# AV of batch 0 over two banks, batch 1's inputs in another order, and five small loads inside a tanh loop: a fused pooling attention and MLP

One core of one Trainium2 chip. The metric is device time in microseconds (us) of one execution.

## The reference

```python
def _attn_ref(q, k, v):                      # [8, 8, 576, 64] float32
    k_p = k.reshape(B, H, Sp, 8, D).mean(axis=3)      # 576 keys pooled to 72
    v_p = v.reshape(B, H, Sp, 8, D).mean(axis=3)
    scores = np.matmul(q, k_p.transpose(0, 1, 3, 2)) / np.sqrt(D)
    attn = softmax(scores)
    return np.matmul(attn, v_p)

def _moe_ref(x, w_in, w_out):                # x [4608, 512], w_in [512, 2048], w_out [2048, 512]
    h = x @ w_in
    return (h - np.tanh(h)) @ w_out
```

The attention's output, heads put side by side, is x. (The softmax is written out in the full reference.)

## The kernel before

TensorE (PE) is the bound. Tokens go through the MLP in nine groups of 512. A group is 64 "h" matmuls (each of 16 tiles: four matmuls, a tanh on ScalarE, a subtraction on VectorE) and 64 "o" matmuls. The attention of batch b + 1 is threaded between the o matmuls of earlier groups; batch 0's stands alone in front. Words used below: AV is the product of attention weights and v; a *turn* is a transpose on PE; a *bank* is a piece of PSUM, where matmuls leave their result (one h tile, 512 float32 columns, fills one in this kernel); the *q tail* is the last 64 rows of a batch's q, *leftovers* are the last 16 of the 144 rows in which k and v are laid out, and both are loaded apart from the main part; kd is the pooled k. The *granted clock* is the share of TensorE's full clock that the profile records as granted. The parts that matter (lines starting with `# ...` stand for code left out):

```python
# GpSimd's stream: the weights, by quarters (w1 all four, w2 two of four)
for c in range(4):
    load_w1(c)
load_w2(0)
nc.gpsimd.tensor_copy(out=v_bf[:, NM, :], in_=v_raw[1][:, NM, :])
load_w2(1)
# ... memsets ...
q_raws[1] = raw.tile([128, H, R + 1, D], FP32, name="q_raw", tag="q_raw")
after(load_k(1), w1_dmas[1])     # SP's stream: batch 1's k, once w1's second quarter is there
load_q(1, False)                 # q without its tail of 64 rows
load_main(v_pairs, v_raw[1], 1, 0, NM)
# ... batch 0: k pooled, q turned, scores, v pooled ...
load_left(v_pairs, v_raw[1], 1, nc.scalar)    # ScalarE's stream: batch 1's v leftovers (four loads)
load_q_tail(1, q_raws[1], nc.scalar)          # and q tail (one load)
# ... AV of batch 0: eight halves of one bank, then the opening of h ...
for i in range(5, NHID):         # the h loop of group 0
    mlp_h(0, i, gts)             # four matmuls, tanh (ScalarE), subtraction (VectorE)
    # ... tail of batch 0's attention at i = 7, 9, 11, 13
pool_k(1, nc.gpsimd, mid=(2, 3)) # w2's quarters 2 and 3 are issued in the middle
after(load_k(2), w2_dmas[2])     # SP's stream: batch 2's k, once w2's third quarter is there
load_v(2)
load_q(2)
# ... the o loop of group 0, with batch 1's attention in it
```

One half of AV in batch 0: three matmuls into one bank, a reciprocal over 4 columns, a product over 256.

The softmax here doesn't subtract the row's maximum and nothing guards it: scores larger than these inputs give would overflow.

## Time and profile before

| | before |
|---|---|
| time, median (range) | 300.62 us (300.56 to 300.81), 3 runs |
| profiled span, granted TensorE clock | 299.1 us, 1.00 |
| PE busy | 291.5 us |
| batch 0's q tail on PE | 26.02 us |
| first o matmul | 34.55 us |
| batch 1's k turned | 37.82 us |

The last three are starts on PE, from its timeline; the prediction shows the lines of the last two. From the third on PE is never without work until the tail of the kernel, so whatever delays one of them delays the end. One more view: ScalarE's timeline in the front. Columns: start, length, engine (ACTq is ScalarE's sequencer issuing a transfer), line, operation, and in brackets the idle time before it with what ended it.

```profile
13.23 1.76 ACTq L106 DMA_DIRECT2D v_raw<-in_v_dram  x4
16.28 0.62 ACTq L127 DMA_DIRECT2D q_raw<-in_q_dram  x1
...
21.90 3.21 ACT L439 ACTIVATE t_sb<-hT_ps 128x512 f32<-128x512 f32 x6 [0.26 <-PE hT_ps L428]
```

The five small loads are issued at 13.23 to 16.9 us, before the tanh work begins. None waits for a large transfer. But one does wait: the first four are issued by 15.0, the fifth only at 16.28. In the built program it waits for batch 0's q tail (128 KB, issued at 8.12, landed 8.1 us later), and the first copies of a turned x, which stand behind it on ScalarE, start at 16.95, 1.0 us after PE has turned the first (15.99).

### The profile page before, as it was taken

How to read it: one execution, taken by the hardware profiler on the slowest of the kernel's cores; microseconds unless marked ns; L12 is line 12 of the kernel's file. 1: busy time of each engine (PE TensorE's matmuls, PEld its weight loads, DVE VectorE, ACT ScalarE, POOL GpSimd, SP SyncE). 2: the span in 40 equal slices, each digit the busy share in tenths (PEclk: the TensorE clock that was granted, in tenths of full speed). 3: DMA queues.
4: the chain of work that ended last, by engine and by line, in shares of the span. 5: the costliest groups of instructions: out<-in, count | busy, mean ns of one | idle time of the engine just before them, and what ended most of it. 6: DMA issues, size and time to landing. Idle time of an engine off the chain costs nothing.

```text
span 299.1 us, 4694 instructions
## 1 busy us (share of the span) xinstructions
PE 291.5 (97%) x1671; PEld 142.5 (48%) x1671; DVE 159.1 (53%) x343; ACT 149.4 (50%) x283; POOL 115.5 (39%) x110
## 2 busy tenths in 40 slices
PE   7989999999999999999999999999999999999994
PEld 3454455544544454445444554455445544444443
DVE  5658665673547444753476247716680758108600
ACT  4647583666146633654265516650665166126511
POOL 8500904871496109922971089307940000000000
PEclk9999999999999999999999999999999999999999
DMA  7999999849854998699648974897431430111032
GB/s 251 226 211 278 311 227 310 263 87 328 234 113 99 271 297 134 117 302 245 107 88 235 300 167 94 242 294 159 97 66 35 95 92 0 37 70 36 0 72 70
DMA packets 66183, 49.79 MB, mean 166 GB/s; under 512 B 39920, under 2 KB 52976, under 8 KB 66160
## 3 DMA queue, kind: packets, MB, share of 16 engines
q1 hardware_dynamic: 58832, 42.94, 56.0%
q0 software_dynamic: 4752, 4.72, 9.4%
q10 hardware_dynamic: 2576, 1.84, 2.3%
q8 instruction: 13, 0.21, 0.3%
q14 instruction: 10, 0.08, 0.1%
HBM read 36.70 MB, written 9.44 MB: 154 GB/s over the span
## 4 chain that ended last, share of the span: by engine, by line
PE 85%; DMA 9%; POOL 4%; issue 0%; SPq 0%; ACT 0%; DVE 0%; POOLq 0%
PE o_ps L456 40%; PE hT_ps L428 37%; DMA w1b<-in_moe_w_in_dram 4%; PE x_ps L346 4%; DMA k_raw<-in_k_dram 4%; PE s_ps L298 3%; POOL k_raw L198 1%; DMA out_dram<-o_sb 1%; POOL k_raw L203 1%; POOL kd L206 1%; POOL w2b L510 0%; PE xT_ps L390 0%; POOL v_raw L576 0%; PE qT_ps L171 0%; POOL w1b L503 0%
## 5 line engine op out<-in xcount | busy, mean ns | idle before, releaser
L456 PE MATMUL o_ps<-w2b,gT 128*128 128x512 bf16 x560 | 134.4, 380 | 0.0
L441 DVE TENSOR_TENSOR gT<-hT_ps,t_sb 128x512 bf16<-128x512 f32 x144 | 98.9, 691 | 57.7 <-ACT t_sb L439 57.6
L428 PE MATMUL hT_ps<-xT,w1b 128*128 128x512 bf16 x576 | 126.9, 379 | 0.3 <-ACT xT L397 0.3
L439 ACT ACTIVATE t_sb<-hT_ps 128x512 f32<-128x512 f32 x144 | 85.6, 597 | 38.3 <-PE hT_ps L428 37.5
L428 PEld LDWEIGHTS <-w1b 128*128 128x128 bf16 x576 | 55.9, 98 | 66.5 <-issue 0.4
L456 PEld LDWEIGHTS <-gT 128*128 128x128 bf16 x560 | 52.5, 98 | 52.0 <-issue 1.4
L465 ACT COPY o_sb<-o_ps 128x512 f32<-128x512 f32 x33 | 19.3, 585 | 75.2 <-PE o_ps L456 75.2
L359 DVE RECIPROCAL rden<-x_ps 128x4 f32<-128x4 f32 x80 | 14.2, 177 | 52.5 <-PE x_ps L346 52.0
L360 DVE TENSOR_TENSOR x_sb<-x_ps,rden 128x256 bf16<-128x256 f32 x80 | 34.0, 425 | 3.5 <-DMA xT<-x_sb 0.6
L148 POOL CAST q_bf<-q_raw 128x2048 bf16<-128x2048 f32 x6 | 11.3, 1888 | 59.9 <-issue 34.8
L198 POOL TENSOR_TENSOR k_raw<-k_raw 128x1280 f32<-128x1280 f32 x7 | 20.2, 2886 | 27.4 <-DMA k_raw<-in_k_dram 16.6
L317 ACT ACTIVATE E<-s_ps 128x288 bf16<-128x288 f32 x60 | 21.4, 410 | 13.2 <-PE s_ps L298 13.0
L346 PE MATMUL x_ps<-VB,E 128*128 128x130 bf16 x240 | 20.8, 221 | 0.4 <-ACT xT L397 0.3
L346 PEld LDWEIGHTS <-E 128*128 128x128 bf16 x240 | 16.9, 98 | 8.8 <-DVE VB L230 0.6
L216 POOL TENSOR_TENSOR v_raw<-v_raw 128x1280 f32<-128x1280 f32 x6 | 17.4, 2898 | 0.0
L298 PE MATMUL s_ps<-qT,KB 128*128 128x288 bf16 (+5 forms) x128 | 17.0, 290 | 0.2
L298 PEld LDWEIGHTS <-KB 128*128 128x128 bf16 (+1 forms) x128 | 7.0, 96 | 10.2 <-issue 3.5
L527 PE MATMUL warm_ps<-xT 128*128 128x512 bf16 x29 | 10.2, 465 | 1.3 <-DVE xT L539 1.3
L206 POOL TENSOR_TENSOR kd<-k_raw 128x640 bf16<-128x640 f32 x7 | 10.8, 1540 | 0.5
L203 POOL TENSOR_TENSOR k_raw<-k_raw 128x640 f32<-128x640 f32 x7 | 10.8, 1541 | 0.5
L397 ACT CAST xT<-xT_ps 128x256 bf16<-128x256 f32 (+1 forms) x14 | 5.8, 436 | 8.5 <-PE xT_ps L390 5.1
L219 POOL TENSOR_TENSOR v_raw<-v_raw 128x640 f32<-128x640 f32 x6 | 9.3, 1544 | 0.5
(73 smaller groups left out, 100.7 us busy)
## 6 DMA issues: line engine op xcount, KB each, us to landing
k_raw<-in_k_dram SPq DMA_DIRECT2D x7, 1024.0 KB, 5.9
q_raw<-in_q_dram SPq DMA_DIRECT2D x7, 1024.0 KB, 10.2
v_raw<-in_v_dram SPq DMA_DIRECT2D x7, 1024.0 KB, 9.3
out_dram<-o_sb SPq DMA_DIRECT2D x38, 128.0 KB, 2.4
out_dram<-o_sb SPq DMA_DIRECT2D x16, 256.0 KB, 3.7
w1b<-in_moe_w_in_dram POOLq DMA_DIRECT2D x4, 512.0 KB, 14.2
w2b<-in_moe_w_out_dram POOLq DMA_DIRECT2D x4, 512.0 KB, 16.9
k_raw<-in_k_dram SPq DMA_DIRECT2D x7, 128.0 KB, 5.8
```

What stands on the lines that cost most here:

```text
L198: first = eng.tensor_tensor(out=r[:, :, 0:4, :], in0=r[:, :, 0:4, :], in1=r[:, :, 4:8, :], op=ALU.add)
L216: eng.tensor_tensor(out=r[:, :, 0:4, :], in0=r[:, :, 0:4, :], in1=r[:, :, 4:8, :], op=ALU.add)
L298: nc.tensor.matmul(dst[p : p + w], lhsT=KB[b % 2][:, o : o + w], rhs=qTs[b][:, m, c0:c1], start=True, stop=True,)
L317: nc.scalar.activation(out=E[:, t, half * hs : (half + 1) * hs], in_=ps[:, :], func=ACT.Exp, scale=SCALE)
L346: nc.tensor.matmul(ps[:, 2 * n : 2 * n + 2, :].rearrange("p h d -> p (h d)") if n < 2 else ps.rearrange("p (a s) d -> p a s d", s=2)[:, :, ...
L359: nc.vector.reciprocal(out=rden[:, :, :], in_=ps[:, :, D:D1])
L360: nc.vector.tensor_tensor(out=x_sb[:, half, :, :], in0=ps[:, :, 0:D], in1=rden[:, :, :].to_broadcast([128, 4, D]), op=ALU.mult,)
L428: nc.tensor.matmul(h_tiles[i][:, :], lhsT=w1b[:, fb, i * 128 : (i + 1) * 128], rhs=xT[:, fb, tok0 : tok0 + TG], start=(fb == 0), stop=(fb ...
L439: nc.scalar.activation(out=t_sb[:, :], in_=h_ps[:, :], func=ACT.Tanh)
L441: nc.vector.tensor_sub(out=gT[:, :], in0=h_ps[:, :], in1=t_sb[:, :])
L456: nc.tensor.matmul(o_ps[:, :], lhsT=gts[i][:, tb * 128 : (tb + 1) * 128], rhs=w2b[:, i, :], start=(i == 0), stop=(i == NHID - 1),)
L465: (nc.vector.tensor_copy if g == 0 and tb % 2 else nc.scalar.copy)(out=o_sb[:, :], in_=o_ps[:, :])
```

## The change

Its intent: spend fewer VectorE instructions in batch 0's AV, which sets the pace of the front; ask for batch 1's k earlier and let no w2 transfer slow it; and take the five small loads off ScalarE where ScalarE now has part of the v pooling and the turns of x to do. Cut to its core (PSUM is also taken as one tile with banks given out by hand, which adds no instruction):

```diff
 # AV of batch 0: two blocks per step, over two banks; v placed by halves (VectorE, ScalarE)
-    av_half(0, 0, 0, xs[0], ps_all)          # eight of these, one bank each
+    av_pair(0, 0, 0)                         # four of these: 6 matmuls into two banks,
+                                             # one reciprocal (8 columns), one product (512)
-    x_pe_transpose(0, 0, xs[0], (0, 2))      # eight, each with a copy of 256
+    x0_turn((0, 1), 0, 7, nc.scalar.copy)    # two blocks per copy
 # batch 1's inputs
     for c in range(4):
         load_w1(c)
-    load_w2(0)
-    load_w2(1)
-    after(load_k(1), w1_dmas[1])
+    k1 = load_k(1)
+    after(k1[:1], w1_dmas[0])
+    load_w2(0)
+    after(w2_dmas, k1[0])                    # w2 held until batch 1's k is there
+    load_w2(1)
+    pool_k(1, nc.gpsimd)
+    load_w2(2)
+    load_w2(3)
 # five small loads of batch 1
-    load_left(v_pairs, v_raw[1], 1, nc.scalar)
-    load_q_tail(1, q_raws[1], nc.scalar)
     for i in range(5, NHID):
         mlp_h(0, i, gts)
+        if i in (5, 7, 9, 11):
+            load_left(v_pairs, v_raw[1], 1, nc.scalar, ((i - 5) // 2,))
+        if i == 13:
+            load_q_tail(1, q_raws[1], nc.scalar)
-    pool_k(1, nc.gpsimd, mid=(2, 3))
     after(load_k(2), w2_dmas[2])
```

## The prediction

> **What bounds the kernel now.** I read the page first: PE is busy for 291.5 of 299.1 us at full granted clock, so only PE's idle stretches and the work that fills time (the warm-up matmuls) can give anything back. Then the chain of waits in order of time, to see where the end is set by something other than PE:
>
> ```profile
> 5.17 0.69 POOL w1b L503
> 5.86 12.86 DMA w1b<-in_moe_w_in_dram
> 18.73 0.38 SPq L102
> 19.21 10.84 DMA k_raw<-in_k_dram
> 30.21 2.90 POOL k_raw L198
> 33.11 1.47 POOL w2b L510 x2
> 34.58 1.58 POOL k_raw L203
> 36.23 1.55 POOL kd L206
> 37.82 0.45 PE kT_ps L259 x5
> ```
>
> Columns are start, length, and what. From 37.82 us to the end the chain is PE alone, piece touching piece. So the change can move only what lies before 37.82, and the end moves by as much as that point moves. The chain there is a chain of transfers: second quarter of w1 landed (18.73), batch 1's k asked for, landed at 30.1, pooled on POOL with two w2 issues in the middle, and only then can PE turn k. The timeline of PE shows how little PE loses there:
>
> ```profile
> 20.41 5.78 PE L428 MATMUL hT_ps<-xT,w1b 128*128 128x512 bf16 x26
> ...
> 34.55 2.75 PE L456 MATMUL o_ps<-w2b,gT 128*128 128x512 bf16 x12
> 37.82 0.45 PE L259 MATMUL kT_ps<-ident,kd 128*128 128x128 bf16 x5 [0.52 <-POOL kd L206]
> ```
>
> The wait for kd is 0.52 us, all that the k part can return by itself. The other candidate is the time before 20.41, where PE reaches its unbroken run of h matmuls: there the chain of batch 0's attention (k, scores, v, AV, turned x) sets the pace, and the timeline of DVE shows AV as eight pairs of a reciprocal and a product:
>
> ```profile
> 14.13 0.76 DVE L230 TENSOR_TENSOR VB<-v_ps,mask 128x256 bf16<-128x256 f32 x2 [0.81 <-PE v_ps L618]
> 15.00 0.18 DVE L359 RECIPROCAL rden<-x_ps 128x4 f32<-128x4 f32 x1
> 15.22 0.42 DVE L360 TENSOR_TENSOR x_sb<-x_ps,rden 128x256 bf16<-128x256 f32 x1
> ...
> 19.63 0.43 DVE L360 TENSOR_TENSOR x_sb<-x_ps,rden 128x256 bf16<-128x256 f32 x1
> ```
>
> DVE is nearly full from 15.00 to 18.93, then waits 0.47 us and ends AV at 20.06. The last thing to read is how long weights take, by the view of the tile w2b:
>
> ```profile
> L510 POOL DMA_DIRECT2D w2b<-in_moe_w_out_dram x4: 747/764/780, 8.1 to 33.8; - x4
> ...
> DMA to landing us min/median/max: 8.7/16.9/24.4
> ```
>
> (issue times in ns, first and last start, then the time to landing). Asked in narrow windows about each issue, the view of transfers gives each landing: w1's quarters land 10.3, 12.9, 15.5 and 19.1 us after their issue, so at 15.46, 18.73, 22.1 and 26.5; w2's at 31.4, 35.7, 41.8 and 44.3. The first quarter of w2 lands 3.2 us before the o stage asks for it at 34.55.
>
> **What the Trainium skill says.** "DMA: Bandwidth & Descriptors", section Queues, rings and completion order: each DMA engine serves the queues it has work for in turn, packet by packet. The trace agrees: counting packets per us, the weight queue has 170 to 205 when alone, and 94 beside 94 of k's 2 KB packets from 24 to 28 us. So k does not overtake w1; it halves it. The same page, Specifications, gives first-byte latencies of about 0.6 us (SP, ACT) and 1 us (POOL); the trace does not agree here: k asked for at 18.73 moves its first bytes at 22.8 (4.1 us), and the third w2 quarter, issued at 33.05, at about 37.4 (4.3 us). I use the trace's. "VectorE: DVE Perf Modes", section on the TRN2 errata, gives a read of PSUM 120 + N cycles at 0.96 GHz: 392 ns for 256 elements, 658 for 512; the trace has 425 and 691. So a product over two banks saves one fixed share. "PSUM — Partial Sum Buffer", the section on bank collisions, asks for semaphores by bank; the built program agrees in that the first AV pair (banks 0 and 1) waits for ScalarE, which still reads half of v in bank 1.
>
> **The change part by part.**
>
> AV on DVE: removed 8 x (177 + 425) ns, added 4 x (about 180 + 691). With the gaps of the timeline one old half takes 0.545 us from start to start, one new pair about 0.90, so 4.36 becomes 3.6 us. The wait of 0.47 before the eighth goes too, since before the last pair PE has only one turn of x to do.
>
> Start of AV: the pooled v in halves lets DVE place the first half while PE pools the second; ScalarE places the second in two activations of 128 elements (estimate 0.25 us each, from 0.37 for 256 and 0.58 for 512). But E of the leftover rows is now computed after the first v half: scores at about 13.0, its exp over at about 14.0, ScalarE's two v pieces at 14.55. First AV pair done 14.95, against 15.00 for the first old half. Nothing gained at the start; the halves only make up for waiting on two blocks. DVE then ends AV at about 18.6 instead of 20.06.
>
> Turning x: ACT evacuates three tiles (two of 512, one of 256) and DVE one, where ACT had eight of 256. That is off the path.
>
> The opening of h: five tiles open with two matmuls each (10 x 0.216 us). The order is now 3, 4, two turns, 2, 0, 1. Tile 4 needs the second quarter of w1, which lands at about 18.6 as before. So 4 opens at 18.6 to 19.0, the turns take 0.25, three tiles 1.3: the openings are done at 20.55, and the remaining 22 matmuls before batch 0's q tail take 4.75, which puts the q tail at 25.3. Before, the timeline of PE has it at 26.02. **AV and opening give 0.7 us**, and PE would be ready for o at 33.85 instead of 34.55.
>
> Batch 1's inputs: k is now asked for after the first quarter of w1 (15.46), so 3.3 us earlier, moves from 19.5, shares with w1 at 94 packets per us, and its 512 main packets are through at 25.0, landed (1 us later, as in the trace) at 26.0. The last quarter of w1 lands at about 27.2 (26.5 before); it is asked for near 29.5, so no wait. POOL issues two w2 quarters from 26.0 and pools k in 6.1 us from 27.5 to 33.7: kd is ready before PE turns k, and the 0.52 us are gone.
>
> The price: the first quarter of w2 is issued at 26.0 instead of 8.05. Its bytes move from 26.0 + 4.3 = 30.3. The SP queue holds behind k the q of batch 1 and, newly, all of its v, because v's issue no longer waits for k to land. Counting packets from 19.5: q's 1024 small ones end at about 29.1 (122 per us beside w1, 338 alone), v has sent 230 by 30.3, its other 282 and w2's first 282 take 3.0 us at 94 each, and w2's last 230 take 1.2 alone: 34.5, landed near **35.4**. PE is ready at 33.85, so this is a new wait of 1.55 us. Then 12 o matmuls (2.59) and k is turned at 38.05, against 37.82: a loss of 0.2 us, the AV gain wholly hidden.
>
> The small loads of v's leftovers and q's tail go into ScalarE's h stretch, one issue of 0.43 us beside a tanh of 0.60 in periods of 0.87; PE has three banks there, so I give them 0 to 0.2 us.
>
> **The rivals.**
>
> First, w2 in time. The path through the w2 landing is long and each part is uncertain: if SP's latency falls to 2 or 3 us because the weight queue is shorter, k lands near 24.5, w2 moves from 28.5 and shares with q instead of v, and lands near 33.7. Then neither wait is there: 0.7 + 0.52 = 1.2 us faster, 299.4. For it speaks that someone chose this order on purpose; against it that all three transfers issued beside a deep weight queue took about 4 us to begin.
>
> Second, w2 later still, at 36.5, if the transfers share worse than counted: 1.3 us slower, 301.9.
>
> Third, the front gains nothing because opening tile 4 so early puts PE behind the second w1 quarter, or gains more (1.5 us) if v's halves start AV earlier. While w2 is late neither shows in the time.
>
> A fourth, PE losing its clock in the longer idle, I hold unlikely: the view by windows grants 1.00 in every stretch of before, and the new idle is under 2 us.
>
> **Range and chances.** I weigh the late w2 (300.6 + 0.2 = 300.8, spread 0.9) at 0.6 and w2 in time (299.4) at 0.4: 0.6 x 300.8 + 0.4 x 299.4 = 300.2. Range 299.0 to 301.6. A change of 2% is 6 us; the whole stretch that can move has 0.52 us of k wait and a front of 20 us whose chain stays, so faster 0.01, same 0.98, slower 0.01.
>
> **What would show it.** The chain of waits should name w2b's transfer between 26 and 35.5 in place of k_raw and POOL; the wait for kd should be gone; the first o matmul should start after 35, with idle before it put down to the w2b transfer; the q tail should start near 25.3; DVE's last AV product should end near 18.6. If the first o matmul starts at 33.9 with no idle, the first rival holds. The prediction is wrong if w2 lands before 33 or after 37, if PE stalls in the h stretch on w1 or on tanh, or if the time after the turn of k is no longer PE alone.

## The result and the profile after

Measured: **325.41 us** median (324.61 to 326.33, 4 runs) against 300.69 (300.56 to 300.81, 4 runs) before. The ratio is 1.082, with a 95% interval of 1.079 to 1.086. Ratios here are the mean time of one kernel's fast runs over that of the other's of the same rounds, so not quite the ratio of the medians. The prediction was 300.2 (299.0 to 301.6) with slower at 1%: wrong.

The profiled span is 322.9 us at a mean clock of 0.966, 23.8 us over before. PE's timeline shows where most of it sits:

```profile
25.28 1.02 PE L460 MATMUL PS<-xT,w1b 128*128 128x512 bf16 x4
48.48 1.86 PE L460 MATMUL PS<-xT,w1b 128*128 128x512 bf16 x4 [22.17 <-DVE gT L473]
...
57.73 2.54 PE L488 MATMUL PS<-w2b,gT 128*128 128x512 bf16 x11
```

PE stops in the middle of group 0's h tiles for 22.17 us, at 26.3. The first o matmul starts at 57.73 in place of 34.55, so 23.2 us of the 23.8 arise before it. The bracket names a VectorE subtraction: the next h tile has no free bank. The view of waits takes it back a step:

```profile
DVE gT L473 <- ACT t_sb L471: 81.8, 133, 22.5
...
ACT t_sb L471 <- DMA k_raw<-in_k_dram: 23.0, 1, 23.0
PE PS L460 <- DVE gT L473: 22.2, 1, 22.2
```

Columns: who waited for whom, us in total, how often, the longest. VectorE waited 22.5 us for one tanh, and that tanh waited 23.0 us, once, for a **k load**. A tanh reads no k. ScalarE's timeline shows what stands before it in ScalarE's stream:

```profile
46.65 0.36 ACTq L129 DMA_DIRECT2D v_raw<-in_v_dram  x1
47.10 1.09 ACT L471 ACTIVATE t_sb<-PS 128x512 f32<-128x512 f32 x2 [22.97 <-DMA k_raw<-in_k_dram]
50.60 0.32 ACTq L129 DMA_DIRECT2D v_raw<-in_v_dram  x1
```

The first small load goes out only at 46.65 and the second at 50.60; the tanhs behind each in ScalarE's stream start only after it, at 47.10 and 51.03. The chain of waits continues from the second one:

```profile
41.72 8.87 DMA v_raw<-in_v_dram
...
50.60 0.32 ACTq L129
```

The k load that ended at 46.6 was issued on SP, by the sync engine's timeline, at 41.02 (5.6 us to landing by the view of transfers):

```profile
41.02 0.58 SPq L134 DMA_DIRECT2D k_raw<-in_k_dram  x1
```

The v load at 41.72 landed at 41.72 + 8.87 = 50.6. Both are **batch 2's**. Its k is held until w2's third quarter has landed, at 40.5, and its v stands behind k in SP's stream. So a small load of batch 1 waited for large loads of batch 2.

The built program says why. Each transfer issued by SP or ScalarE signals its landing on one of eight semaphores, handed out in turn along one list of all engines' instructions. Each landing adds 16, and a transfer is issued only once its semaphore's previous user has landed (by a wait of its own, unless an earlier wait already covers it). This is the part of the list that matters, read from the built program of after (not a profile):

```
issuer   load                            signals   first waits for
SP       batch 2, k, 128 rows            DMAHW4    ... third w2 quarter
ScalarE  batch 0, q tail                 DMAHW5
SP       batch 2, k, remaining rows      DMAHW6
SP       batch 2, v, 128 rows            DMAHW7
SP       batch 2, v leftovers (4 loads)  DMAHW0 to 3
SP       batch 2, q (2 loads)            DMAHW4, 5
ScalarE  batch 1, v leftover 0           DMAHW6    DMAHW6 >= 32: batch 2's k remaining rows
ScalarE  batch 1, v leftover 1           DMAHW7    DMAHW7 >= 32: batch 2's v
ScalarE  batch 1, v leftover 2           DMAHW0    DMAHW0 >= 48: batch 2's v leftover
ScalarE  batch 1, v leftover 3           DMAHW1    DMAHW1 >= 48: batch 2's v leftover
ScalarE  batch 1, q tail                 DMAHW2    DMAHW2 >= 48: batch 2's v leftover
```

In the text of the kernel the small loads come before batch 2's. In this list they come behind. The Trainium skill, "DMA: Bandwidth & Descriptors", section on why a DMA increments its semaphore by 16, explains what the wait is for: with two transfers in flight on one semaphore, part of one's signals can pass for the other's. It asks for "One semaphore per in-flight slot, not one per stream." The waits in this program keep that rule, and the trace shows what they cost.

The rest of the 23.8 us. From q tail to first o, before takes 34.55 - 26.02 = 8.53 us and after 57.73 - 25.04 = 32.69: 24.16 more, 22.17 of which is the stop. The clock record of the trace shows most of the other 2.0: the clock is at half from 31.3, within the stop, for 20.48 us. The page's slices (8.07 us each) show it:

```profile
PE   7992009989999999999999999999999999999995
...
PEclk9999557999999999999999999999999999999999
```

PE works at half rate from 48.48 to 51.8, which costs 1.7 us. Some 0.3 us is not accounted for. The q tail is 1.0 us earlier in this run; that takes the 24.16 to the 23.2. Past the first o, before's wait of 0.52 us for k is gone and 1.09 us of waiting for a VectorE product is new (below), which makes the 0.6.

The other lines that answer to the prediction's. The last product of AV in VectorE's timeline, and the view of the tile w2b:

```profile
17.61 0.69 DVE L705 TENSOR_TENSOR x<-PS,rden 128x512 bf16<-128x512 f32 x1
```

```profile
L542 POOL DMA_DIRECT2D w2b<-in_moe_w_out_dram x4: 751/760/787, 25.5 to 33.9; - x4
...
DMA to landing us min/median/max: 7.4/9.6/11.7
```

AV ends at 18.3 and w2 is issued from 25.5, both as planned. Neither can show in the time behind such a stop.

### The profile page after: what moved, and what is told of

Its sections match the earlier page's. It is cut to its first block, busy times and chain, and to the rows that moved or that the text cites. A ratio compares the mean times of both kernels' runs of the same rounds, so it can differ in the third digit from the quotient of the medians.

```text
span 322.9 us, 4724 instructions
## 1 busy us (share of the span) xinstructions
PE 292.8 (91%) x1681; PEld 143.3 (44%) x1681; DVE 162.7 (50%) x335; ACT 149.0 (46%) x281; POOL 116.1 (36%) x110
## 4 chain that ended last, share of the span: by engine, by line
PE 78%; DMA 6%; DVE 4%; ACT 1%; issue 0%; SPq 0%; ACTq 0%; DVEq 0%
PE PS L488 36%; PE PS L460 35%; PE PS L387 4%; DMA v_raw<-in_v_dram 3%; DMA w2b<-in_moe_w_out_dram 3%; PE PS L328 2%; DVE VB L270 1%; DMA out_dram<-o_sb 1%; DVE VB L251 1%; DVE v_raw L237 0%; DVE gT L473 0%; PE PS L423 0%; ACT t_sb L471 0%; DVE x_sb L373 0%; DVE v_raw L240 0%
## 5 line engine op out<-in xcount | busy, mean ns | idle before, releaser
L460 PE MATMUL PS<-xT,w1b 128*128 128x512 bf16 x576 | 128.3, 382 | 22.3 <-DVE gT L473 22.2
L473 DVE TENSOR_TENSOR gT<-PS,t_sb 128x512 bf16<-128x512 f32 x144 | 98.8, 690 | 81.9 <-ACT t_sb L471 81.8
L488 PE MATMUL PS<-w2b,gT 128*128 128x512 bf16 x560 | 134.3, 379 | 0.0
L471 ACT ACTIVATE t_sb<-PS 128x512 f32<-128x512 f32 x144 | 85.4, 597 | 63.4 <-PE PS L460 37.1
L497 ACT COPY o_sb<-PS 128x512 f32<-128x512 f32 x33 | 19.3, 585 | 75.2 <-PE PS L488 75.2
L372 DVE RECIPROCAL rden<-PS 128x4 f32<-128x4 f32 x72 | 12.7, 177 | 50.1 <-PE PS L387 49.8
L373 DVE TENSOR_TENSOR x_sb<-PS,rden 128x256 bf16<-128x256 f32 x72 | 30.5, 424 | 2.7 <-DMA xT<-x_sb 0.2
L347 ACT ACTIVATE E<-PS 128x288 bf16<-128x288 f32 x60 | 21.4, 410 | 13.2 <-PE PS L328 13.0
L387 PE MATMUL PS<-VB,E 128*128 128x130 bf16 x240 | 20.5, 220 | 1.3 <-DVE VB L270 1.1
L328 PE MATMUL PS<-qT,KB 128*128 128x288 bf16 (+5 forms) x128 | 17.2, 292 | 0.2
L328 PEld LDWEIGHTS <-KB 128*128 128x128 bf16 (+1 forms) x128 | 7.2, 97 | 10.5 <-issue 4.1
```

Of the source, the lines that this page charges most:

```text
L328: nc.tensor.matmul(dst[p : p + w], lhsT=KB[b % 2][:, o : o + w], rhs=qTs[b][:, m, c0:c1], start=True, stop=True,)
L347: nc.scalar.activation(out=E[:, t, half * hs : (half + 1) * hs], in_=ps[:, :], func=ACT.Exp, scale=SCALE)
L372: nc.vector.reciprocal(out=rden[:, :, :], in_=ps[:, :, D:D1])
L373: nc.vector.tensor_tensor(out=x_sb[:, half, :, :], in0=ps[:, :, 0:D], in1=rden[:, :, :].to_broadcast([128, 4, D]), op=ALU.mult,)
L387: nc.tensor.matmul(ps[:, 2 * n : 2 * n + 2, :].rearrange("p h d -> p (h d)") if n < 2 else ps.rearrange("p (a s) d -> p a s d", s=2)[:, :, ...
L460: nc.tensor.matmul(h_tiles[i][:, :], lhsT=w1b[:, fb, i * 128 : (i + 1) * 128], rhs=xT[:, fb, tok0 : tok0 + TG], start=(fb == 0), stop=(fb ...
```

## The experiments

**Theory A**: the moved small loads wait, by shared semaphores, for batch 2's large loads, which are themselves held by w2; the rest of the change is worth some tenths. **Rival B**: the late w2 is the cause (the hold slows the whole front and the small loads only happen to be seen there). **Rival C**: the place of the loads on ScalarE, among the tanhs, is bad whatever they wait for. Ten kernels were run, one of them twice; all gave correct results. The second and third sets were made to split what remained once A was settled. The runs of before on the same chips had medians of 301.2 (11 runs), 301.0 (11) and 300.9 (9).

### First set: whose load is waited for?

**The list turned round.** The small loads stay where the change put them. Batch 2's k gets one more wait, for batch 1's q tail, which puts it behind the small loads in the list:

```diff
-        eng.dma_start(                       # in load_q_tail
+        return eng.dma_start(
-            load_q_tail(1, q_raws[1], nc.scalar)
+            q1_tail = load_q_tail(1, q_raws[1], nc.scalar)
-    after(load_k(2), w2_dmas[2])
+    k2 = load_k(2)
+    after(k2, w2_dmas[2])
+    after(k2, q1_tail)
```

> The changed kernel with one wait more: batch 2's k load waits also for batch 1's q tail. In the built program this moves batch 2's loads behind ScalarE's five small loads in the handing out of the completion semaphores, so that those five wait for loads long landed (batch 0's, batch 1's k) and not for batch 2's. Theory A (the five loads wait for the previous user of their semaphore, batch 2's k and v, and hold ScalarE for 23 us): the idle of 22.2 us before the h matmul disappears, the first small load is issued near 22.5 us instead of 46.65, and the time falls to about 300.4 (299 to 302); what is left above the old sum is the first quarter of w2, landing near 35.5. Rival B (ScalarE's loads are slow to issue in the middle of the tanh loop, or a transfer of batch 1 itself is late, or the two-bank tiles hold each other): one more wait cannot help; 325 or more.

Measured: 302.2 us median (302.08 to 303.81, 6 runs), ratio 1.005 (1.003 to 1.007). In the built program the small loads now wait for batch 0's loads and, the last two, for batch 1's k, all landed before they are issued. The time is just above the range expected. PE's timeline and ScalarE's:

```profile
36.40 4.44 PE L488 MATMUL PS<-w2b,gT 128*128 128x512 bf16 x11 [2.20 <-DMA w2b<-in_moe_w_out_dram]
```

```profile
24.11 0.35 ACTq L129 DMA_DIRECT2D v_raw<-in_v_dram  x1
...
31.86 0.62 ACTq L150 DMA_DIRECT2D q_raw<-in_q_dram  x1
...
39.91 0.62 ACT L175 CAST q_bf<-q_raw 64x512 bf16<-64x512 f32 x1 [3.19 <-DMA q_raw<-in_q_dram]
```

The same five loads at the same places, each issued beside a tanh. The stop is gone, and 23 of the 24.7 us with it. That is theory A, shown; the hold of w2 is still there, so B is out as the main cause. What B keeps is the 2.20 us of waiting for w2 before the first o.

**The small loads on GpSimd**, ahead of the held weights. GpSimd's loads signal on eight other semaphores of their own, which they share with w1 and w2:

```diff
+    load_left(v_pairs, v_raw[1], 1, nc.gpsimd)
     q_raws[1] = raw.tile(...)
+    load_q_tail(1, q_raws[1], nc.gpsimd)
-        if i in (5, 7, 9, 11):               # and the two lines of i == 13
-            load_left(v_pairs, v_raw[1], 1, nc.scalar, ((i - 5) // 2,))
```

> The changed kernel with the five small loads of batch 1 issued by POOL ahead of the w2 quarters, none by ScalarE. Theory A: no wait of ScalarE on a load is left, 300.4 us (299 to 302), first o matmul near 35.5 and put down to w2b's landing (the step of the prediction on w2, alone). Rival B1 (the AV part or the hold of w2 itself costs the 25 us): stays above 315. Rival B2 (w2 is in time): first o matmul at 33.6 without idle, 299.3.

Measured: 304.46 us (303.58 to 304.74, 5 runs), ratio 1.010 (1.009 to 1.012). No stop in the h tiles here either; the q tail waits 0.95 us for a w1 quarter on GpSimd, which has nothing else to do then. The time is above the range expected: PE waits 2.68 us for w2 before the first o (36.58), and in all five runs the mean clock is 0.992 to 0.994.

**Batch 2's k not held by w2**: if A holds, the small loads then wait for a k that comes sooner.

```diff
-    after(load_k(2), w2_dmas[2])
+    load_k(2)
```

> The changed kernel, with batch 2's k no longer held until the third w2 quarter is there; nothing about ScalarE's loads is touched. Theory A: ScalarE's first small load is issued the moment that batch 2's k has landed, now near 40 us instead of 46.6, the second when batch 2's v has, near 45.5 instead of 50.6; the time falls by about 5.5 us to 319.5 (316 to 322.5). Rival B (the stall has to do with batch 1's transfers, w2 or PSUM): batch 2's k only adds traffic, 325 or slower, and the first small load does not follow k's landing.

Measured: 321.23 us (320.45 to 321.96, 4 runs), ratio 1.066. ScalarE's timeline:

```profile
40.95 0.35 ACTq L129 DMA_DIRECT2D v_raw<-in_v_dram  x1
41.40 1.09 ACT L471 ACTIVATE t_sb<-PS 128x512 f32<-128x512 f32 x2 [16.56 <-DMA k_raw<-in_k_dram]
```

The list is the same; only k's own hold was taken away. Its remaining rows are now issued on SP at 25.33 and land 15.6 us later (the view of that load), at 40.9; the first small load goes out at 40.95. So what ScalarE waits for moves with the k transfer, and ends with its landing. It is not a fixed cost of an issue.

**The moved loads alone, in the kernel before**:

```diff
-    load_left(v_pairs, v_raw[1], 1, nc.scalar)
-    load_q_tail(1, q_raws[1], nc.scalar)
     for i in range(5, NHID):
         mlp_h(0, i, gts)
+        if i in (5, 7, 9, 11):
+            load_left(v_pairs, v_raw[1], 1, nc.scalar, ((i - 5) // 2,))
+        if i == 13:
+            load_q_tail(1, q_raws[1], nc.scalar)
```

> The kernel before with one part of the change alone: the five small loads moved from before AV into the tanh loop of group 0. In the built program the second of them then waits for batch 1's k (landed near 29.4 us), the third for batch 1's v (near 39). Theory A: ScalarE stands until about 39 at the third load, PE with it, 312 us (309 to 315). Rival B (placement in the loop costs only the issue): 300.6 to 301.

Measured: 315.5 us (313.44 to 315.85, 4 runs), ratio 1.046; above the range, and 3.5 us over the 312 expected. ScalarE's timeline:

```profile
29.04 0.33 ACTq L106 DMA_DIRECT2D v_raw<-in_v_dram  x1
29.47 1.09 ACT L439 ACTIVATE t_sb<-hT_ps 128x512 f32<-128x512 f32 x2 [2.55 <-DMA k_raw<-in_k_dram]
...
40.03 0.44 ACT L334 ACTIVATE E<-s_ps 128x320 bf16<-128x320 f32 x1 [9.47 <-DMA v_raw<-in_v_dram]
```

The loads alone, with no hold of w2, cost 14 us. In this program's list the small loads share with batch 1's k and v, and those are what is waited for. Against my expectation there is one more wait behind it: the q tail is now issued at 44.29, and its cast waits 4.41 us more.

### Second set: what is left once the stop is gone?

**The hold alone, in the kernel before** (small loads on GpSimd, so that they share with no load that is held back):

```diff
-    load_w2(0)                               # and load_w2(1), further down
+    load_left(v_pairs, v_raw[1], 1, nc.gpsimd)
+    load_q_tail(1, q_raws[1], nc.gpsimd)
-    after(load_k(1), w1_dmas[1])
+    k1 = load_k(1)
+    after(k1[:1], w1_dmas[0])
+    load_w2(0)
+    after(w2_dmas, k1[0])
+    load_w2(1)
+    pool_k(1, nc.gpsimd)
+    load_w2(2)
+    load_w2(3)
-    load_left(v_pairs, v_raw[1], 1, nc.scalar)
-    load_q_tail(1, q_raws[1], nc.scalar)
-    pool_k(1, nc.gpsimd, mid=(2, 3))
```

> The kernel before with the hold of w2 alone (k after the first w1 quarter, w2 after k), the five small loads issued by POOL so that no semaphore order of ScalarE's comes in. Theory A2: PE is ready for o at 34.5 us, the first w2 quarter lands near 36.5, the clock halves for a window, k is turned near 40.5 instead of 37.82: 2.7 us slower than the kernel before (1.3 to 3.3; 1.3 if the clock holds). Rival (the hold returns the 0.52 us wait for kd, w2 in time): 0.4 us faster.

Measured: 303.7 us (302.39 to 304.38, 6 runs), ratio 1.008 (1.005 to 1.011), as expected. PE's timeline:

```profile
37.27 4.39 PE L456 MATMUL o_ps<-w2b,gT 128*128 128x512 bf16 x12 [2.98 <-DMA w2b<-in_moe_w_out_dram]
```

Twelve o matmuls take 2.75 us in before and 4.39 here. The clock record of this run has half clock from 37.2 for 3.413 us; the view by windows, 34 to 42 us, gives a mean of 0.79. The runs fall in two groups: 302.4 to 303.2 at a mean clock of 1.00, and 304.2 to 304.4 at 0.994. The runs of the list turned round do too: 302.08 to 302.22 at 0.999 to 1.00, and 303.71 and 303.81 at 0.994. So a PE wait of 2 to 3 us costs itself and is followed, in some runs, by a half clock worth some 1.6 us. That the wait brings the half clock is not shown: two runs with matmuls put into the wait, below, lost the same.

**AV alone, in the kernel before** (all of the AV part; k and w2 as before; small loads on GpSimd). From the changed kernel:

```diff
-    k1 = load_k(1)                           # and the hold, as the change added it
-    after(k1[:1], w1_dmas[0])
+    after(load_k(1), w1_dmas[1])
+    pool_k(1, nc.gpsimd, mid=(2, 3))         # behind the h loop, w2 issued as before
+    load_left(v_pairs, v_raw[1], 1, nc.gpsimd)
+    load_q_tail(1, q_raws[1], nc.gpsimd)     # both lines gone from the h loop
```

> The kernel before with the AV part alone (two-bank tiles, v by halves, the new order of openings), k and w2 as before, the five small loads issued by POOL. The front should gain 0.7 to 1.0 us (batch 0's q tail at 25.0 to 25.3 instead of 26.02), but kd still comes at 37.8 us, so PE waits for it 1.3 to 1.5 us instead of 0.52 and the time stays: 0.0 us (-0.3 to +0.3) against the kernel before, unless the longer idle halves the clock, then 1 us slower. Rival (the end follows the front): 0.9 us faster.

Measured: 300.4 us (300.17 to 300.46, 5 runs), ratio 0.998 (0.995 to 1.000). PE's timeline:

```profile
37.08 0.44 PE L291 MATMUL PS<-ident,kd 128*128 128x128 bf16 x5
```

The first o matmul starts at 34.49 and k is turned at 37.08 instead of 37.82, without a wait. The expected wait for kd of 1.3 to 1.5 us did not come, and the time is below the range: k, asked for at 18.70 as in before (18.73), landed by 29.4 and not 30.1. So this is not AV alone. The five small loads have left ScalarE too, and no run moves them to GpSimd by themselves; which of the two gives the 0.2% is open.

**First w2 quarter not held** (on top of the list turned round): it goes out right behind w1, the other three quarters stay held.

```diff
     for c in range(4):
         load_w1(c)
+    load_w2(0)
-    load_w2(0)
-    after(w2_dmas, k1[0])
     load_w2(1)
+    after(w2_dmas[1:], k1[0])
```

> As k2_after_tail (one wait more, semaphores in the good order), and the first quarter of w2 issued right behind w1 as in the kernel before; the other three stay held until batch 1's k is there. Theory A2 (with ScalarE's stall gone, what is left above the kernel before is the late first w2 quarter and the clock lost in waiting for it): first o matmul at about 34.1 us without idle, granted clock 1.00 in the stretch, kd there before it is wanted, k turned near 36.8 us instead of 37.82: 1.0 us faster than the kernel before (0.4 to 1.5). Rival (the AV part costs as much as it gains, or w2 ahead of k delays k): within 0.2 us of the kernel before or slower.

Measured: 304.13 us (303.04 to 305.94, 6 runs), ratio 1.010 (1.007 to 1.014). The expectation failed: I had taken w2 for the only wait left. Three of the six runs, 304.83 to 305.94, also had a clock of 0.989 to 0.994. PE's timeline of the profiled one (303.15):

```profile
42.86 0.38 PE L328 MATMUL PS<-qT,KB 128*128 128x512 bf16 x1 [2.89 <-ACT qT L119]
```

The wait for w2 is gone (the first o matmul starts at 34.50) and k is turned at 37.09 without a wait, but PE then waits 2.89 us for a turned q (no half clock follows in this run). ScalarE's timeline tells why: its cast of q waits 4.37 us for the q tail, issued inside the loop at 32.31 and landed 9.4 us later. This wait was there before too, beside the wait for w2 (3.19 us on ScalarE in the list turned round, above). It is what rival C is right about: even with no semaphore in the way, the loop is too late a place for the q tail, though it costs PE 2.89 us here and not 22.

**The wait for w2 filled** with ten warm-up matmuls (on top of the list turned round), to keep the clock:

```diff
+    warm_pe(10)                              # ahead of the o loop
```

> As k2_after_tail, with ten warm-up matmuls of zeros in PE's wait for the first w2 quarter (ten of 0.216 us, 2.2 us, into a bank that the second o tile clears). If the half clock that k2_after_tail had for 3.4 us after that wait comes from PE's idle, the clock stays at 1.00, the first twelve o matmuls take 2.6 us and not 4.4, and the time is 1.7 us under k2_after_tail (1.2 to 2.0), so about that of the kernel before. If the clock falls for another reason (load on the chip, the time since the start), the time is that of k2_after_tail.

Measured: 302.86 us (302.21 to 304.74, 6 runs), ratio 1.007 (1.004 to 1.011). In the profiled run the clock stays at 1.00 over the wait and twelve o matmuls take 2.75 us. Four of six runs lie at 302.2 to 303.2 with a clock of 0.998 to 0.999, two at 304.7 with one of 0.993 to 0.994. The gain of 1.2 to 2.0 us that was expected did not come: against before on its own chip the ratio is no better than the 1.005 of the list turned round. So the profiled run fits the idea that the wait brings the half clock, and the two slow runs, with the same ten matmuls in the wait, speak against it, unless w2 came later in them than these lasted (they were not profiled). One of the 31 runs of before (302.65, at 0.994) lost clock as well. What sets it off stays open.

### Third set: is a version faster than before?

**Both waits avoided**: the changed kernel with the small loads on GpSimd, early, and the first w2 quarter not held.

```diff
+    load_w2(0)                               # right behind w1
+    load_left(v_pairs, v_raw[1], 1, nc.gpsimd)
+    load_q_tail(1, q_raws[1], nc.gpsimd)
-    load_w2(0)
-    after(w2_dmas, k1[0])
+    after(w2_dmas[1:], k1[0])                # behind load_w2(1) to load_w2(3) as before
-        # the five small loads in the h loop
```

> The changed kernel with the five small loads of batch 1 issued by POOL at about 13 to 19 us (q's tail too, which the tail_w2first run had land at 41.7 us, so that PE waited 2.9 us for ScalarE behind it), and the first w2 quarter issued right behind w1; the rest of the hold kept. If the small loads in ScalarE's loop and the late first w2 quarter are all that the change costs, nothing waits between 20 and 45 us: no idle of PE over 0.3 us there, clock 1.00 in nearly all runs, 0.7 us under the kernel before (0.3 to 1.2). If the hold costs something else, it is at or above the kernel before.

Measured: 300.52 us (300.37 to 300.86, 5 runs), ratio 0.999 (0.998 to 1.001). PE's timeline:

```profile
36.34 0.44 PE L289 MATMUL PS<-ident,kd 128*128 128x128 bf16 x5
...
39.36 1.02 PE L488 MATMUL PS<-w2b,gT 128*128 128x512 bf16 x4 [1.23 <-DMA w2b<-in_moe_w_out_dram]
```

Here the front is won: the first o matmul starts at 33.75 and k is turned at 36.34, 1.5 us before the kernel before. 1.23 us of it go to a wait for the second w2 quarter, which the expectation (no idle over 0.3 us) had not seen. The gain of 0.1% is some 0.3 us, the least that was expected, and the interval includes none.

**AV alone, again** (the same kernel, on the chip of the third set):

> The same kernel as av_alone, on the same chip as the run beside it, to see whether its 0.7 us under the kernel before stands (0.4 to 1.0) and whether the hold of w2's last three quarters adds or takes anything (within 0.3 us of the run beside it).

Measured: 300.57 us (300.39 to 300.85, 5 runs), ratio 0.999 (0.998 to 1.000): 0.3 us under before, short of the 0.4 expected. The two best versions are equal, and within 0.1 to 0.2% of the kernel before: no version that is clearly faster was found.

**The small loads back at their old place**, the rest of the change kept:

```diff
     v_main_act(VB[0], v_b, 2, 4)
+    load_left(v_pairs, v_raw[1], 1, nc.scalar)
+    load_q_tail(1, q_raws[1], nc.scalar)
-        # the five small loads in the h loop
```

> The changed kernel with the five small loads put back on ScalarE where the kernel before has them, ahead of AV. In the built program they then use the semaphores after batch 1's k (main and dense part), q and v, in this order. Theory A: ScalarE stands from about 14.4 us, takes the loads one by one as k lands (25.6), k's dense part (26.3), q (29.7) and v (34), and turns the first x at about 34.6 instead of 16.3: 18 us late, of which the waits for w2 and kd are hidden, with a half-clock window on top: 318.5 us (316 to 321). Rival (the loop is the wrong place and the old place is free): 300 to 302.

Measured: 322.79 us (321.76 to 323.4, 4 runs), ratio 1.073; above my range. ScalarE's timeline:

```profile
25.28 11.24 ACTq L129 DMA_DIRECT2D v_raw<-in_v_dram  x4
...
37.23 1.07 ACT L727 CAST xT<-PS 128x512 bf16<-128x512 f32 x2 [22.80 <-issue]
```

The first load goes out when batch 1's k has landed (25.3) and the fourth when its v has; in this program's list they share with batch 1's k (two loads), q and v. So the old place is not safe either: in before the same lines, at the same place, waited only for batch 0's q tail, to 16.28. What changed is which loads stand ahead of them in the list, and on which semaphores: batch 1's v and batch 2's k and v stood behind them in before and stand ahead of them here. That asking for batch 1's inputs earlier did this is my reading; it was not tested alone. PE waits 20.12 us for ScalarE's copy of x.

## Why the prediction was wrong

**The step that failed** is "The small loads of v's leftovers and q's tail go into ScalarE's h stretch, one issue of 0.43 us beside a tanh of 0.60 [...] so I give them 0 to 0.2 us." It counted what an issue takes and not what it waits for. The issue did take 0.32 to 0.63 us. Its waits took 22.97 us on ScalarE and 22.17 on PE, and moving batch 2's k behind the small loads in the list, all else kept, took 23 us away. The waits stood in the built program before the run, and the trace of before had one of their kind (the fifth small load, held to 16.28). None of the four rivals had it, which is why the range was narrow and slower stood at 1%. One of the signs that the prediction named for being wrong did come: PE stalled in the h stretch on a tanh.

**The hold of w2** was sized too small and the mechanism right. First w2 landing: predicted near 35.4; in after 25.54 + 10.0 = 35.5, though there the stop is under way; in the list turned round 25.9 + 10.5 = 36.4. The steps before it held too (k landed at 25.5, predicted 26.0; kd ready at 33.1, predicted 33.7). But the loss was given as 1.55 us of idle and 0.2 us net; where it can be seen, the idle is 2.20, 2.68 and 2.98 us, for w2 starts the o stage at 36.4 to 37.3 rather than 35.4, and the hold alone costs 2.4 us by its ratio of 1.008. One of its inputs was loosely read: the 4.3 us that the third w2 quarter took to begin are not all latency, for its queue still moved the second quarter's packets until 35.2 (they started at 33.05 and 37.1). And of "all three transfers" that took about 4 us to begin, the prediction shows two.

**AV and the opening**, predicted 0.7 us: the mechanism holds, AV ends on VectorE at 18.3 (predicted 18.6). The gain at the point where PE could start o (34.55 in before) is 0.05 to 0.8 us in the traces: 34.50 and 34.49 in two of them, 34.20 (36.40 less 2.20), 33.90 (36.58 less 2.68) and 33.75. In the time it is 0.1 to 0.2%, at the edge of what 5 runs show, and the small loads' move to GpSimd is in it. The front's start varies by as much from run to run: the q tail starts on PE between 25.04 and 26.27 in nine traces with the new front and between 25.60 and 26.12 in three with the old one (before, hold_alone, only_loads), and hold_alone, with the old front, could have started o at 34.29 (37.27 less 2.98). So neither the 0.7 us nor the 1.0 us of after's one trace is shown to be the change's.

**The fourth rival**, a lost clock, was dismissed and was real: half clock for 20.48 us in and after the long stop, and in a part of the runs 3.413 us after a wait of only 2.2 to 3.0.

**Not foreseen at all**: while GpSimd cast q and pooled v, two VectorE products for batch 1 grew. VectorE's timeline of after:

```profile
64.76 2.30 DVE L251 TENSOR_TENSOR VB<-v_raw,mask 128x512 bf16<-128x512 f32 x1
66.98 3.69 DVE L270 TENSOR_TENSOR VB<-v_raw,mask 128x256 bf16<-128x256 f32 x1
```

The same two take 0.69 and 0.42 us in before. PE waited 1.09 us for the second. GpSimd cast q from 64.63 to 66.52, and pooled v from 67.50 to 70.38. The kept traces go further than this one: the two products are at 2.30 to 2.31 and 3.68 to 3.69 us in the three traces in which GpSimd's cast starts some 0.12 us before the first of them (after, k2_free, loads_early), and at 0.69 and 0.42 us in the other ten, in which GpSimd runs nothing beside them. No experiment moved GpSimd's work alone.

So the time went, by the trace: 22.17 us to the stop, some 1.7 to the half clock behind it, 1.09 to the slow product, some 0.3 unexplained; less about 1.0 in the front and 0.52 at k.

## What to carry to other kernels

A load put into an engine's stream is not only an issue of 0.3 to 0.6 us: it can carry a wait for whichever load had its completion semaphore before, and everything behind it on that engine waits along. So whenever a change moves loads or changes what they wait for, list each load's semaphore and its previous user in the built program, not in the text, and look whether that user lands late; do it most of all for an engine that feeds the bound one. Here the small loads did least harm early on GpSimd: there too they waited for a large load, a w1 quarter, by 0.95 to 2.29 us each, but that one was not held and nothing urgent stood behind them.

## What the Trainium skill lacked or had wrong

- No page tells that a build may hand a few completion semaphores to the loads of several engines in turn, so that a small load of one batch waits for a large load of a later one: 22.97 us here, 16.56 with batch 2's k released earlier, none with the list turned round. "DMA: Bandwidth & Descriptors", section on why a DMA increments its semaphore by 16, gives the rule that makes such a wait necessary, not its cost.
- "DMA: Bandwidth & Descriptors", Specifications: the first-byte latencies of about 0.6 us (SP) and 1 us (GpSimd) were longer here while other loads were under way: batch 1's k moved its first packets 4.0 us after its issue in before (18.73 to 22.7) and 3.6 us in after (15.24 to 18.8), and the first w2 quarter 4.2 us in after (25.54 to 29.8; its queue still carried the last w1 quarter until 27.3). What makes them longer was not tested.
- "TensorE: Matmul & The Clock Gate", Part 1, What's actually happening: it gives a return to half clock after at least one idle window of about 3.4 us. Here waits of 2.20, 2.68 and 2.98 us were followed by a half clock of 3.413 us, and one of 2.89 us was not; it came in some runs of a kernel and not in others of the same kernel, at 1.6 us each, and in two with ten matmuls put into the wait. The same section says that the window runs free of the kernel, so that the slow matmuls at a kernel's start vary in number from run to run; a like variation showed here, in mid-kernel.
